# Queries taken from the key products, kept in DRAM, and three more exp buffers in a two-layer attention kernel

## The chip, the core and the metric

The kernel runs on one core of one Trainium2 chip. The metric is the device time of one execution in microseconds; 1635.77 us is the median of three runs of the kernel before.

## What is computed

Two layers, each an attention block and a feed-forward block on the same weights, with x of 2048 rows of 512 values in bf16:

```python
x = A_x
x = x + _A_ref(_layernorm(x, axis=-1), A_wqkv, A_wo)
x = x + _B_ref(_layernorm(x, axis=-1), B_w1, B_w2)
x = x + _A_ref(_layernorm(x, axis=-1), A_wqkv, A_wo)
x = x + _B_ref(_layernorm(x, axis=-1), B_w1, B_w2)
```

`_A_ref` is full softmax attention with 32 heads of 16 dimensions and no mask: scores are q k^T / 4, 2048 by 2048 for each head, then the product with v, then the output weights wo. `_B_ref` is x w1 (512 to 1792), silu, and w2 back to 512.

## The kernel before, in words

**Tiles and segments.** The heads are taken in 8 blocks (`hb`) of four, the queries in 4 chunks (`c`) of 512. A *segment* is one chunk of queries for one head block in one layer. Its work is cut into tiles of 128 keys (`kt`) by two heads by 512 queries: a score matmul pair writes a PSUM slot of 128x1024 (L1244; there are three slots), an exp takes the slot to an SBUF buffer in bf16, and value matmuls (L1320) add the buffer into the PSUM bank of the segment. There are 74 segments and 2048 tiles. Layer 1 starts on its first two chunks before the last quarter of the keys exists: kinds "old" (24 tiles) and "new" (8 tiles) share the work of a chunk, and the "old" sum is kept and rescaled by `f_piece` when the "new" part is done.

**Two ways to do an exp.** ScalarE (ACT) does it in one activation (L1459). VectorE (DVE) does it by bits: a tensor_scalar that writes 16-bit integers that read as bf16 (L1489), and three more copies of these shifted by constants, whose average is close to the exp. The shifts are done by GpSimd (POOL, L1550) or at times by DVE (L1523). A tile that DVE takes holds four buffers and needs four value products instead of one.

**Who orders the work.** A planner in the kernel's own Python code (`Flow`) plays the engines' clocks with fixed costs and writes the order of PE, ACT, DVE and POOL out; the chip follows that order, with semaphores where one engine needs another. `want_dve` gives a tile to DVE only if enough exp buffers are free (`spare`), not too many shifts are in arrears (`behind`), not too many rows wait for their value product (`ROWS`), and DVE is not late (`LATE`). The five thresholds `spare, many, few, behind, hurry` come from a table `KINDS` with a letter for each setting; `RULES` gives a letter to every stretch of 16 tiles. Work other than scores and values (projections, feed-forward, layer norms) is cut into `Piece`s, lists of steps with an engine, a cost and a due time, in four queues. Steps named "sp" are issued as soon as what they follow is done, and their DMAs land on the planner's clock after `T_ISSUE` and `T_LAND`. `warm` lets PE do matmuls on idle data (L1355) where its busy share in the last 3.3 us would fall below 0.65. DMAs on SP's queue are issued in the program's order.

**Exp buffers.** `bufs` holds NB = 11 of them; `lent` adds storage that is idle for a while: the four pairs of `q_old` and eight pieces of layer 1's value rows early in layer 0 (given back at segments 8, 15, 16, 24 and 32), the idle hidden tile for a few segments, and twelve more from segment 59 on.

**Keys and queries.** `wkq` holds the weights of keys and queries woven head by head: 16 columns of keys, then 16 of queries. A key product (`k_piece`, four steps of four matmuls, L306) takes 128 of these columns, so that its PSUM bank holds, for each of the four heads, 16 rows of keys and 16 rows of queries. `k_out` (L315) keeps the keys, multiplies the query rows by zero, and adds a row of ones:

```python
nc.vector.tensor_scalar(
    out=KT[:, hb, c * 512 : (c + 1) * 512], in0=ps,
    scalar1=own, scalar2=onescol, op0=ALU.mult, op1=ALU.add,
)
```

A query product (`q_mm`) takes the same columns moved on by 16, so that the queries fall on the keys' rows. `q_own` (L381) masks it into `qc`, `q_abs` (L388) takes absolute values, `q_abs_bias` (L396) makes a weight from the largest keys, a bias product on PE (`q_bias`) turns them into a bound on each score, and `q_sum` (L405) writes query and bound to the tile that the scores read. These steps are one chain: only one segment's chain runs at a time. `q_old` keeps the queries of the "old" segments (and those of layer 0's last chunk, made a chunk ahead) for the "new" ones; `q_again` (L454, L464) makes the new query tile from it.

**Transposes** of outputs and activations are DMAs on SP's queue (`turn`, L234).

Of the kernel before, what the change touches and what calls it, by code (L numbers as in the profile page):

```python
# [20 lines left out]
def kernel(  # L21
# [16 lines left out]
    P = 128  # L38
# [24 lines left out]
    NB = 11  # L63
# [12 lines left out]
    small = ctx.enter_context(tc.tile_pool(name="small", bufs=2))  # L76
    spool = ctx.enter_context(tc.tile_pool(name="spool", bufs=3, space=bass.MemoryType.PSUM))
# [96 lines left out]
    KT = xpool.tile([P, HB, S], BF16, name="KT")  # L174
    amax = xpool.tile([P, HB, NQC], FP32, name="amax")
# [3 lines left out]
    q_old = xpool.tile([P, HB, 512], BF16, name="q_old")  # L179
    q_more = xpool.tile([P, 512], BF16, name="q_more")  # L180
# [5 lines left out]
    q_mores = [q_more[:], v_flat[:, 1024 * HB : 1024 * HB + 512]]  # L186

# [3 lines left out]
    def q_kept(seg):  # L191
        return q_old[:, seg.hb, :] if seg.c != 1 else q_mores[MORE.index(seg.hb)]
# [37 lines left out]
    turns = [0]  # L230

    def turn(out, in_):
        turns[0] += 1
        nc.sync.dma_start_transpose(out=out, in_=in_)  # L234

# [8 lines left out]
    class Piece:  # L244
        def __init__(self, steps, after=None, lag=0):
            self.steps, self.lag = list(steps), lag
            self.after = list(after) if isinstance(after, (list, tuple)) else [after] * (after is not None)
            self.due = 0
            self.chain = None
# [129 lines left out]
    def q_own(ps):  # L379
        qc = qwork.tile([P, 512], BF16, name="qc", tag="qc")  # L380
        nc.vector.tensor_scalar(  # L381
            out=qc[:], in0=ps, scalar1=own, scalar2=None, op0=ALU.mult
        )
        return qc
# [38 lines left out]
    def q_pieces(seg, after):  # L423
        cell = {}

        def c1():
            cell["qc"] = q_own(cell["ps"][:, :])

        def c2():
            cell["qu"] = q_abs(cell["qc"])  # L430

        def d():
            bank(cell, "q_ps")
            q_bias(cell["bm"], cell["ps"][:, :], cell["qu"])

        def e():
            dst = q_kept(seg) if seg.keep else q_tile()
            q_sum(cell["ps"][:, :], cell["qc"], dst)
            seg.QT = dst

        first = Piece(four(
            lambda cts: q_mm(seg.c, seg.hb, cell["ps"][:, :], cts),
            lambda: bank(cell, "q_ps"),
        ) + [dve(750, c1, "c"), dve(302, c2, "l")])
        bm = bound(seg, cell, after)
        last = Piece([pe(MM, d, "o"), dve(700, e, "c")], [first, bm])
        return chained(first, bm, last, cell)

    def q_again(seg, after):
        cell = {}  # L450

        def a():
            cell["q"] = q_tile()
            nc.vector.tensor_scalar(  # L454
                out=cell["q"].bitcast(I16), in0=q_kept(seg).bitcast(I16),
                scalar1=0x7FFF, scalar2=None, op0=ALU.bitwise_and,
            )

        def b():
            bank(cell, "q_ps")  # L460
            q_bias(cell["bm"], cell["ps"][:, :], cell["q"])

        def e():
            nc.vector.tensor_tensor(  # L464
                out=cell["q"], in0=cell["ps"][:, :], in1=q_kept(seg), op=ALU.add
            )
            seg.QT = cell["q"]

        first = Piece([dve(302, a, "l")])
        bm = bound(seg, cell, after)  # L470
        last = Piece([pe(MM, b, "o"), dve(700, e, "c")], [first, bm])
        return chained(first, bm, last, cell)

    def f_piece(seg, after):

        cell = {}

        def a():
            cell["ps"] = narrow("f_ps")
            mm(cell["ps"][:, :], sel[:, 0, :], seg.QT, True, False)  # L480

        def b():
            mm(cell["ps"][:, :], sel[:, 1, :], q_kept(seg), False, True)
# [11 lines left out]
        return Piece([pe(MM, a, "o"), pe(MM, b), act(T_TANH, e, "c"), dve(690, m, "l")], after)  # L495
# [146 lines left out]
    def ending(oT, attn, slots, units):  # L642
# [90 lines left out]
        def hidden(f2):  # L733
            if f2 % 2 == 0:
                w = wide("h2_ps") if f2 else first
                pss = [w[:, i, :] for i in range(2)]
            else:
                pss = [p.tile([P, 512], FP32, name="h3_ps", tag=t)[:, :] for p, t in pools]
            for i in range(2):
                h_mm(c, 2 * f2 + i, pss[i], range(CT))  # L740
            for i in range(2):
                k = 2 * ((2 * f2 + i) % 4)
                t_sb = q_old[:, k : k + 2, :].bitcast(FP32).rearrange("p a b -> p (a b)")
                h_out(hT, 2 * f2 + i, pss[i], h_tanh(pss[i], t_sb))
# [21 lines left out]
    class Seg:  # L766
        def __init__(self, L, c, hb, kind):
# [3 lines left out]
            self.keep = kind == "old" or (L, c) == (0, NQC - 1)  # L771
# [36 lines left out]
    def old_keys(hb):  # L808
        new = [k_piece(c, hb) for c in range(NQC - 1)]
        for c, p in enumerate(new):  # L810
            p.after = [normed[c]] * (normed[c] is not None)
        first, rest = q_pieces(segs[NQC * HB + hb], None)
# [5 lines left out]
        rest[0].after = [parts[-1]]  # L818
        return [new[0], new[1], parts[0], first, new[2]] + parts[1:] + rest

    def prep(t):

        seg = segs[t]
        if seg.kind == "new" and seg.c == 1:
            first, rest = q_again(seg, None)
            return [first] + rest + [f_piece(seg, rest[-1])]
        if seg.kind == "new":
            new = []
            last = v_end[0] if v_end else None
            first, rest = q_again(seg, None)  # L830
            if seg.hb > 0:
                new = [k_piece(NQC - 1, seg.hb)]
# [4 lines left out]
            rest[0].after = [new[-1]]  # L837
            return [first] + new + rest + [f_piece(seg, rest[-1])]
        if seg.L == 0 and seg.c == 0:
            new = [k_piece(c, seg.hb) for c in range(NQC)]  # L840
            first, rest = q_pieces(seg, None)
# [6 lines left out]
            rest[0].after = [parts[-1]]  # L848
            return [new[0], new[1], parts[0], first, new[2], parts[1], new[3], parts[2], parts[3]] + rest
        if seg.kind == "old" and seg.c == 0:  # L850
            return old_keys(seg.hb) if seg.hb == HB - 1 else []
        first, rest = q_pieces(seg, None)
        return [first] + rest

    def musts(i):

        ts = list(range(i + 1 if i <= n_old else i + 2, i + 2 if i < n_old else i + 3))
        if (segs[i].L, segs[i].c) == (0, NQC - 2):
            ts.append(i + HB)
        last = (NQC - 1) * HB  # L860
        return [
            p for t in ts if t < len(segs) and not (last <= t < last + HB and t != i + HB)
# [6 lines left out]
    k_ns = ns_of([k_piece(0, 0)])  # L869
# [39 lines left out]
    def old_rows():  # L909
        return [q_old[:, 2 * k : 2 * k + 2, :] for k in range(HB // 2)]  # L910

    done = n_old + 2 + 2 * HB
    lent = [
        (0, 2 * HB - 1, spare(old_rows)),
# [5 lines left out]
        (done, 99, spare(old_rows)),  # L920
# [3 lines left out]
    class Flow:  # L924
# [40 lines left out]
        def landed(self, at):  # L965
            n, turns[0] = turns[0], 0
            for _ in range(n):
                start = max(self.sp, at + 100)
                self.sp = start + T_ISSUE
                at = max(at, start + T_LAND)  # L970
            return at
# [3 lines left out]
        def head(self):  # L975

            for q in self.qs:
                while q and not q[0].begun and q[0].steps[0][0] == "dve":
                    self.bg.append(q.pop(0))
            for q in self.qs:  # L980
                if q and q[0].steps[0][0] == "sp" and all(d.done for d in q[0].after):
                    p = q.pop(0)
# [118 lines left out]

        def begin(self, seg):
# [3 lines left out]
            if seg.L == 0 and seg.c == NQC - 1 and seg.hb > 0:  # L1106
                new = due(old_keys(seg.hb - 1), first[NQC * HB + seg.hb - 1])
# [4 lines left out]
            self.qs[0] += v_late * (i == 0) + musts(i)  # L1112
# [17 lines left out]
        def close(self):  # L1130
# [22 lines left out]
            if oT is not None:  # L1153
# [23 lines left out]
                if seg.hb == HB - 1:  # L1177
# [5 lines left out]
                    if seg.L == 0:  # L1183
                        new += next_pieces(seg.c, 1, ln, new[-1])
                        if seg.c == NQC - 1:
                            new.append(k_piece(seg.c, 0))
# [4 lines left out]
                    self.qs[1] += due(new, first[end] - 8)  # L1191
# [397 lines left out]
    RULES = (  # L1589
        "llllllllllllllllwwwwaaaaaaaaaaaaaaaajjjjaaaaaaaabbbbaaaaaaaaaaaa"  # L1590
        "aaaaaaaaaaaaaaaaaaaaaaaaaaaaaaaaffffffffffffffffmmmmmmmmcccccccc"
    )
# [156 lines left out]
```

## Time and profile before

| what | before |
|---|---|
| median of three runs, us | 1635.77 (1634.13 to 1635.88) |
| the profiled execution's own time, us | 1633.4 |
| its span, first to last instruction, us | 1631.6 |
| first score / first exp on ACT, us | 32.1 / 32.7 |
| last exp on ACT ends, us | 1589.1 |
| tiles with their exp on ACT / on DVE | 1625 / 423 |
| shifts on POOL / on DVE | 1155 / 114 |
| DMA transposes on SP | 139 |
| granted TensorE clock | 0.998 |

An engine's busy time on the page is the union of its instructions' times. Matmuls overlap: four of 32 columns run side by side, and the next four start 0.226 us after them, though each is shown with 0.38 us. ACT's exps overlap as well: one is shown with 1.19 us and the next starts after 0.917 us. A row of the groups gives the line, the engine, out<-in by the program's names (with shapes), the count, the busy time and the mean duration, then the engine's idle time just before these instructions and what ended it. A row of a table by stage gives the stretch, its length, then busy time (count) of the instructions asked for, the granted clock, the share of the DMA engines and GB/s.

### The profile page before, as it was taken

What the parts mean: (1) busy time and instruction counts of PE and PEld (TensorE: products, weight loads), DVE (VectorE), ACT (ScalarE), POOL (GpSimd) and SP (SyncE); (2) the same over time, 40 slices, a digit from 0 to 9 for tenths busy, and PEclk for the clock granted to TensorE, in tenths of its full rate; (3) what the DMA queues carried; (4) which work ended last, traced back from release to release, by engine and by line L of the source; (5) the groups of instructions that cost most, each with busy time, mean ns of one, the idle gap of its engine ahead of it and who ended that gap; (6) DMA issues with size and microseconds to landing.
All of it is one profiled execution on the core that took longest, in us unless ns stands there. A gap on an engine that the chain in (4) does not pass through costs nothing.

```text
span 1631.6 us, 42640 instructions
## 1 busy us (share of the span) xinstructions
PE 1558.9 (96%) x17522; PEld 498.3 (31%) x17528; DVE 1177.3 (72%) x1481; ACT 1582.1 (97%) x1796; POOL 1239.4 (76%) x1305
## 2 busy tenths in 40 slices
PE   8999999999999999999999998999999999999998
PEld 3232222223323333233333233222223322333333
DVE  7788888776777767657886557787666787777754
ACT  6999999999999999999999999999999999999993
POOL 3899998886788778766766655877767889889970
PEclk9999999999999999999999999999999999999999
DMA  5000001000110011001000000001000100010010
GB/s 194 5 8 8 8 8 24 15 8 12 28 21 5 8 27 28 5 8 18 21 14 2 1 15 8 11 11 30 17 8 14 24 21 8 12 37 11 8 28 13
DMA packets 85268, 30.80 MB, mean 19 GB/s; under 512 B 76624, under 2 KB 84560, under 8 KB 85072
## 3 DMA queue, kind: packets, MB, share of 16 engines
q1 hardware_dynamic: 83056, 26.99, 7.2%
q8 instruction: 137, 2.24, 0.6%
q10 hardware_dynamic: 2016, 1.08, 0.2%
q14 instruction: 59, 0.48, 0.1%
HBM read 7.86 MB, written 2.10 MB: 6 GB/s over the span
## 4 chain that ended last, share of the span: by engine, by line
PE 59%; ACT 19%; DVE 9%; issue 6%; POOL 5%; DMA 1%; ACTq 0%; DVEq 0%; POOLq 0%
PE slot L1244 20%; PE q_ps L1320 17%; ACT p L1459 13%; PE y_ps L306 7%; PE q_ps L306 3%; POOL p L1550 3%; PE h_ps L306 3%; PE k_ps L306 3%; ACT t_sb L568 2%; DVE p L1489 2%; ACT v L1459 2%; DVE hT L572 1%; PE v_ps L306 1%; POOL v L1550 1%; DVE attn L502 1%
## 5 line engine op out<-in xcount | busy, mean ns | idle before, releaser
L1459 ACT ACTIVATE p<-slot 128x1024 bf16<-128x1024 f32 x1171 | 1166.7, 1191 | 8.7 <-PE slot L1244 7.9
L1550 POOL TENSOR_TENSOR p<-p,steps 128x512 int32<-128x512 int32 x568 | 594.8, 1071 | 229.3 <-DVE p L1489 195.1
L1320 PE MATMUL q_ps<-p,v 128*17 128x512 bf16 x4634 | 527.3, 381 | 5.4 <-POOL p L1550 2.1
L1244 PE MATMUL slot<-QT,KT 32*128 32x512 bf16 x3104 | 439.5, 382 | 22.2 <-ACT p L1459 7.5
L1489 DVE TENSOR_SCALAR p<-slot 128x1024 uint16<-128x1024 f32 x281 | 342.7, 1220 | 118.1 <-PE slot L1244 112.2
L1244 PEld LDWEIGHTS <-KT 32*128 32x128 bf16 x4096 | 190.0, 91 | 579.0 <-issue 572.9
L1459 ACT ACTIVATE v<-slot 128x1024 bf16<-128x1024 f32 x301 | 338.7, 1210 | 1.4 <-PE slot L1244 1.2
L1320 PEld LDWEIGHTS <-v 128*17 128x17 bf16 x6634 | 162.5, 88 | 283.8 <-issue 224.7
L1320 PE MATMUL q_ps<-v,v 128*17 128x512 bf16 x1308 | 201.4, 381 | 1.1 <-DVE oT L1146 0.4
L1550 POOL TENSOR_TENSOR p<-v,steps 128x512 int32<-128x512 int32 x162 | 170.8, 1075 | 26.8 <-DVE v L1489 22.7
L1550 POOL TENSOR_TENSOR v<-p,steps 128x512 int32<-128x512 int32 x127 | 135.3, 1072 | 25.7 <-DVE p L1489 19.8
L1459 ACT ACTIVATE q_old<-slot 128x1024 bf16<-128x1024 f32 x129 | 149.0, 1197 | 0.6 <-PE slot L1244 0.5
L1489 DVE TENSOR_SCALAR v<-slot 128x1024 uint16<-128x1024 f32 x93 | 113.4, 1220 | 39.5 <-PE slot L1244 35.9
L306 PE MATMUL h_ps<-xnT,w_sb 128*32 128x512 bf16 x1568 | 129.0, 384 | 12.7 <-DVE hT L572 9.7
L1244 PE MATMUL slot<-q_old,KT 32*128 32x512 bf16 x896 | 122.7, 382 | 4.6 <-ACT p L1459 2.9
L572 DVE SCALAR_TENSOR_TENSOR hT<-t_sb,h_ps 128x512 bf16<-128x512 f32 x98 | 67.0, 684 | 77.9 <-ACT t_sb L568 77.9
L306 PE MATMUL y_ps<-w_sb,hT 128*32 128x512 bf16 x1568 | 120.4, 382 | 1.0 <-DVE hT L572 0.6
L1320 PE MATMUL q_ps<-q_old,v 128*17 128x512 bf16 x582 | 95.3, 381 | 0.2 <-DVE oT L1146 0.2
L306 PE MATMUL q_ps<-xnT,wkq 128*32 128x512 bf16 x1008 | 82.9, 383 | 2.2 <-DVE hT L572 1.7
L306 PE MATMUL k_ps<-xnT,wkq 128*32 128x512 bf16 x960 | 77.5, 383 | 1.7 <-DVE hT L572 0.7
L568 ACT ACTIVATE t_sb<-h_ps 128x512 f32<-128x512 f32 x98 | 73.9, 754 | 0.0
L1550 POOL TENSOR_TENSOR q_old<-p,steps 128x512 int32<-128x512 int32 x59 | 62.9, 1068 | 13.7 <-DVE p L1489 8.3
(162 smaller groups left out, 1532.2 us busy)
## 6 DMA issues: line engine op xcount, KB each, us to landing
w_sb<-in_B_w_dram SPq DMA_DIRECT2D x2, 1792.0 KB, 12.6
out_dram<-x_sb SPq DMA_DIRECT2D x15, 128.0 KB, 1.7
x_sb<-in_A_x_dram SPq DMA_DIRECT2D x3, 512.0 KB, 6.7
at<-oT SPq DMA_TRANSPOSE x63, 2.3
wraw<-in_A_wqkv_dram SPq DMA_DIRECT2D x2, 432.0 KB, 8.3
xnT<-hT SPq DMA_TRANSPOSE x44, 2.4
wv_sb<-in_A_wqkv_dram ACTq DMA_DIRECT2D x1, 512.0 KB, 6.3
wo_sb<-in_A_wo_dram SPq DMA_DIRECT2D x1, 512.0 KB, 8.2
```

The costliest lines, as they stand in the source:

```text
L306: nc.tensor.matmul(ps[g, :], lhsT=lhsT[:, g], rhs=rhs, start=start, stop=stop, skip_group_check=True)
L502: nc.vector.tensor_tensor(out=attn[:, :, 64 * hb : 64 * hb + DH * n].rearrange("p t (j d) -> p t j d", j=n), in0=at_ps[:, :, :, 0:DH], in1 ...
L568: nc.scalar.activation(t_sb, ps, ACT.Tanh, scale=0.5)
L572: nc.vector.scalar_tensor_tensor(out=hT[:, ft, :], in0=t_sb, scalar=1.0, in1=ps, op0=ALU.add, op1=ALU.mult)
L1244: nc.tensor.matmul(self.slots[k][:, jj, :], lhsT=KT[32 * j : 32 * j + KR, t.seg.hb, t.kt * P : (t.kt + 1) * P], rhs=t.seg.QT[32 * j : 32 * ...
L1320: nc.tensor.matmul(self.o_ps[32 * j : 32 * j + VW, :], lhsT=vs[seg.L][:, t.kt, 4 * seg.hb + j, :], rhs=buf[:, jj, :], start=not seg.opened ...
L1459: nc.scalar.activation(buf[:].rearrange("p a b -> p (a b)"), self.slots[x.slot][:].rearrange("p a b -> p (a b)"), ACT.Exp, scale=float(SCALE),
L1489: nc.vector.tensor_scalar(out=whole.bitcast(U16), in0=self.slots[x.slot][:].rearrange("p a b -> p (a b)"), scalar1=float(UNIT), scalar2=fl ...
L1550: nc.gpsimd.tensor_tensor(out=b1.bitcast(I32), in0=b0.bitcast(I32), in1=steps32[:, k : k + 1].to_broadcast([P, 512]), op=ALU.add,)
```

## The change

- A key product's bank is copied whole to a staging tile. Four DMAs of 16 rows take the keys of the four heads to KT, four more take the queries to a scratch in DRAM (`kept_q`). KT's other rows are filled once, by GpSimd, ahead of its other work (head blocks 1 to 7).
- Query products go, but for head block 0 of layer 0. A segment's chain begins with four loads from the scratch into `qc`, whose other rows stay zero. `q_again` goes: the "new" segments load the same queries again.
- `q_old` and `q_more` go. The finished query tile of an "old" segment is stored to DRAM (`old_q`) and fetched for `f_piece`. Layer 0's last chunk no longer makes its queries a chunk ahead.
- Exp buffers: 14 instead of 11. `q_old` is no longer lent; the value weights (2 buffers, from segment 45) and the woven key and query weights (4, from segment 53) are.
- Every stretch has the setting "a". The planner knows the moves' costs, and DMAs that one step issues no longer wait for each other's landing on its clock.

The core of the diff:

```diff
-    NB = 11
+    M_ISSUE, M_LAND = 100, 2200
+    NB = 14
...
     KT = xpool.tile([P, HB, S], BF16, name="KT")
+    for hb in range(1, HB):
+        nc.gpsimd.tensor_copy(out=KT[:, hb, :], in_=onescol.to_broadcast([P, S]))
...
+    def move(out, in_):
+        turns.append((M_ISSUE, M_LAND))
+        nc.sync.dma_start(out=out, in_=in_)
+
+    def groups(t, lo, cols):
+        return [t[32 * j + lo : 32 * j + lo + DH, cols] for j in range(4)]
...
-    def k_piece(c, hb):
+    def k_piece(L, c, hb):
         cell = {}
-        return Piece(four(
+
+        def out():
+            st = stpool.tile([P, 512], BF16, name="kq", tag="kq")
+            nc.vector.tensor_copy(out=st[:], in_=cell["ps"][:, :])
+            for k_in, k_to in zip(
+                groups(st, 0, slice(0, 512)), groups(KT[:, hb, :], 0, slice(512 * c, 512 * c + 512))
+            ):
+                move(k_to, k_in)
+            for j, q_in in enumerate(groups(st, DH, slice(0, 512))):
+                move(kept_q[L, hb, c, j, :, :], q_in)
+
+        p = Piece(four(
             lambda cts: k_mm(c, hb, cell["ps"][:, :], cts),
             lambda: bank(cell, "k_ps"),
-        ) + [dve(810, lambda: k_out(c, hb, cell["ps"][:, :]), "c")])
+        ) + [dve(700, out, "c")])
...
+        def load():
+            for j, q_to in enumerate(groups(qc, 0, slice(0, 512))):
+                move(q_to, kept_q[seg.L, seg.hb, seg.c, j, :, :])
+
+        if (seg.L, seg.hb) == (0, 0):
+            first = Piece(four(
+                lambda cts: q_mm(seg.c, seg.hb, cell["ps"][:, :], cts),
+                lambda: bank(cell, "q_ps"),
+            ) + [dve(750, c1, "c"), dve(302, c2, "l")])
+        else:
+            first = Piece([("sp", 0, load, "")], made)
+            first.chain = cell
+            first = Piece([dve(302, c2, "l")], first)
         bm = bound(seg, cell, after)
         last = Piece([pe(MM, d, "o"), dve(700, e, "c")], [first, bm])
...
-        (0, 2 * HB - 1, spare(old_rows)),
...
-        (done, 99, spare(old_rows)),
+        (n_old + 4, 99, spare(wv_rows)),
+        (keyed, 99, spare(key_rows)),
...
-    RULES = (
-        "llllllllllllllllwwwwaaaaaaaaaaaaaaaajjjjaaaaaaaabbbbaaaaaaaaaaaa"
-        "aaaaaaaaaaaaaaaaaaaaaaaaaaaaaaaaffffffffffffffffmmmmmmmmcccccccc"
-    )
+    RULES = "a" * (len(tiles) // STRETCH)
```

The letters are, in the order `spare, many, few, behind, hurry`: a (5, 6, 2, 3, 1.0), l (6, 9, 2, 3, 1.0), w (4, 6, 2, 5, 1.0), j (6, 4, 2, 3, 1.0), b (3, 4, 2, 3, 1.0), f (4, 6, 2, 3, 1.0), m (7, 4, 2, 3, 1.0), c (3, 6, 2, 3, 1.0).

More of the change, by code (lines that the diff above doesn't have):

```diff
@@ L436, in e @@
         def e():
[L437 to L444, printed above, removed]
+            seg.QT = q_tile()
+            q_sum(cell["ps"][:, :], qc, seg.QT)
+            if seg.kind == "old":
+                move(old_q[seg.c, seg.hb, :, :], seg.QT)
+        def load():
[10 more added lines that the diff above has]
+            first = Piece([dve(302, c2, "l")], first)
         bm = bound(seg, cell, after)
         last = Piece([pe(MM, d, "o"), dve(700, e, "c")], [first, bm])
[L447 to L456, printed above, removed]
-            )
[L459 to L472, printed above, removed]
+        head = first.after if made is not None else []
+        first, rest = chained(first, bm, last, cell)
+        return head + [first], rest
     def f_piece(seg, after):
@@ L493, in m, with load @@
             seg.scaled = True
-        return Piece([pe(MM, a, "o"), pe(MM, b), act(T_TANH, e, "c"), dve(690, m, "l")], after)
+        def load():
+            move(q_was[:], old_q[seg.c, seg.hb, :, :])
+        fetch = Piece([("sp", 0, load, "")])
+        f = Piece([pe(MM, a, "o"), pe(MM, b), act(T_TANH, e, "c"), dve(690, m, "l")], [fetch, after])
+        fetch.key, f.key = "fetch", "f"
+        return fetch, f
     def heads_norm(at_ps, hb, attn):
@@ L808, in old_keys @@
     def old_keys(hb):
-        new = [k_piece(c, hb) for c in range(NQC - 1)]
+        new = [k_piece(1, c, hb) for c in range(NQC - 1)]
         for c, p in enumerate(new):
             p.after = [normed[c]] * (normed[c] is not None)
-        first, rest = q_pieces(segs[NQC * HB + hb], None)
         parts = [
@@ L817, in old_keys @@
         parts.append(amax_all(hb, 2, parts))
-        rest[0].after = [parts[-1]]
-        return [new[0], new[1], parts[0], first, new[2]] + parts[1:] + rest
+        parts[-1].key = hb
+        return [new[0], new[1], parts[0], new[2]] + parts[1:]
     def prep(t):
@@ L907, in idle_hidden, with wv_rows, key_rows @@
         return [t[:, 2 * k : 2 * k + 2, :] for k in range(FT // 2)]
-    def old_rows():
-        return [q_old[:, 2 * k : 2 * k + 2, :] for k in range(HB // 2)]
+    def wv_rows():
+        assert all((1, tt) in v_made for tt in range(TT))
+        return [wv_sb[:, 2 * k : 2 * k + 2, :] for k in range(CT // 2)]
+    def key_rows():
+        assert with_q[1, NQC - 1, HB - 1].done
+        return [wkq[:, ct, 0 : 2 * D].rearrange("p (a b) -> p a b", a=2) for ct in range(CT)]
     done = n_old + 2 + 2 * HB
+    keyed = max(s.i for s in segs if s.kind == "new" and s.c == 0) + 1
     lent = [
-        (0, 2 * HB - 1, spare(old_rows)),
         (0, HB, spare(rows(x_flat, 0, 3))),
@@ L965, in landed @@
         def landed(self, at):
-            n, turns[0] = turns[0], 0
-            for _ in range(n):
+            land = at
+            for issue, ns in turns:
                 start = max(self.sp, at + 100)
-                self.sp = start + T_ISSUE
-                at = max(at, start + T_LAND)
-            return at
+                self.sp = start + issue
+                land = max(land, start + ns)
+            turns.clear()
+            return land
         def head(self):
             for q in self.qs:
[L978 to L982, printed above, removed]
+                while q:
+                    p = q[0]
+                    if p.steps[0][0] == "dve" and not p.begun:
+                        self.bg.append(q.pop(0))
+                        continue
+                    if p.steps[0][0] != "sp" or not all(d.done for d in p.after):
+                        break
+                    if p.chain is not None and self.chain not in (None, p.chain):
+                        break
+                    q.pop(0)
+                    self.chain = p.chain or self.chain
                     at = max([d.ready for d in p.after] + [min(self.pe, self.act, self.dve)])
@@ L1098, in force, with known @@
                 self.step(p, max(at, getattr(self, p.steps[0][0])))
+        def known(self, pieces):
+            for p in pieces:
+                if p.key == "fetch":
+                    p.after += [with_q[k] for k in ("f",) if k in with_q]
+                if p.key is not None:
+                    with_q[p.key] = p
+            return pieces
         def begin(self, seg):
```

80 lines of the change are left out of this document (42 added, 38 removed).

## The prediction, made before the changed kernel was run

> **What bounds the kernel now.** I read the page's busy line and its costliest groups first, then what ScalarE and VectorE wait for, then the exp instructions by stage.
>
> ```profile
> PE 1558.9 (96%) x17522; PEld 498.3 (31%) x17528; DVE 1177.3 (72%) x1481; ACT 1582.1 (97%) x1796; POOL 1239.4 (76%) x1305
> ...
> L1459 ACT ACTIVATE p<-slot 128x1024 bf16<-128x1024 f32 x1171 | 1166.7, 1191 | 8.7 <-PE slot L1244 7.9
> ```
>
> And from the groups of TensorE alone:
>
> ```profile
> L1355 PE MATMUL q_ps<-wo_sb,wkq 128*16 128x512 bf16 (+1 forms) x175 | 60.6, 379 | 0.0
> ```
>
> Both PE and ACT look full, but they are not full in the same way. L1355 issues matmuls that compute nothing: the planner puts them in where TensorE would otherwise idle. So the busy PE has room, and its chain share (59% of the span) mostly says that it hands ACT its slots on time. ACT has no such filler: before its largest group of exps it idles 8.7 us in 1631.6 us. Exps start on ACT every 0.917 us (mean distance of starts in the trace, gaps over 1.3 us left out). The trace has 1171 + 301 + 129 + 24 = 1625 exps on ACT, and 1625 x 0.917 = 1490 us. The other 423 of 2048 tiles go to DVE (L1489). **The time is therefore the number of tiles left to ACT:** each tile more on DVE is worth 0.92 us, if nobody makes ACT wait.
>
> What sets that number? I cut the trace where the lent exp buffers change (start of segments 8, 16, 24, 32, 42, 59, 66), and asked for L1489 in each stretch. The count in brackets is DVE's tiles.
>
> ```profile
> 32.10:215.50 183.40, 69.46 (x57) 1.00 0.04 7
> 215.50:403.70 188.20, 71.98 (x59) 1.00 0.06 13
> 403.70:601.30 197.60, 62.17 (x51) 1.00 0.09 17
> 601.30:798.60 197.30, 59.80 (x49) 1.00 0.08 16
> 798.60:990.00 191.40, 48.83 (x40) 1.00 0.05 11
> 990.00:1234.00 244.00, 69.42 (x57) 0.99 0.07 14
> 1234.00:1400.20 166.20, 62.23 (x51) 1.00 0.08 17
> 1400.20:1631.60 231.40, 72.04 (x59) 1.00 0.08 19
> ```
>
> The stretches hold 256, 256, 256, 256, 240, 304, 224 and 256 tiles, so DVE's shares are .223, .230, .199, .191, .167, .188, .228, .230. The buffers by the code are 23, 20, 14, 12, 11, 11 (18 for five short segments), 23, 23. The share follows the buffers up to about 20 and then stays. POOL agrees: its passes (L1550) fill 165 of 183 us in the first stretch and 116 of 191 us in the fifth.
>
> **The change, part by part.**
>
> *Buffers.* NB goes from 11 to 14, but q_old no longer lends its four; weights lend two, later six, late in layer 1. By stretch: 22, 19, 17, 15, 14, then 14 to 23 (mostly 16 to 23), then 28 and 28. I interpolate the shares above: 17 buffers lie halfway between 14 (.199) and 20 (.230), so .2145, 55 tiles for 51; 15 buffers .204, 52 for 49; 14 buffers .199, 48 for 40; about 17 buffers in the sixth, .2145, 65 for 57. The first two and the last two are on the flat part: 0. Together 4 + 3 + 8 + 8 = 23 tiles, x 0.92 = **-21 us**. Bounds: 0 (another condition holds DVE back) and 46 tiles, -42 us (all of segments 16 to 58 at .230).
>
> *Query products.* What goes is seen in the groups of TensorE and of VectorE:
>
> ```profile
> L306 PE MATMUL q_ps<-xnT,wkq 128*32 128x512 bf16 x1008 | 82.9, 383 | 2.2 <-DVE hT L572 1.7 <-DVE x_sb L581 0.2 <-DVE QT L405 0.2
> ```
>
> ```profile
> L315 DVE TENSOR_SCALAR KT<-k_ps,cols 128x512 bf16<-128x512 f32 x61 | 49.1, 806 | 13.1 <-PE k_ps L306 12.0 <-PE k_ps L302 0.5
> ...
> L381 DVE TENSOR_SCALAR qc<-q_ps,cols 128x512 bf16<-128x512 f32 x64 | 47.7, 746 | 12.8 <-PE q_ps L306 12.2
> ```
>
> 1008 matmuls are 63 products of 16. Three stay (head block 0 of layer 0), 60 go: 240 groups of four at 0.226 us (start to start in the trace) is 54 us of PE. On DVE 60 x 0.746 = 44.8 us go with L381, and 60 key evictions fall from 0.806 to the 0.69 of a plain copy out of PSUM (L1146: 0.685), 7.0 us. PE's part by itself is worth nothing, since its slack is already filled with idle matmuls. It also covers what more DVE tiles need: three more rows each, half a 0.22 us slot a row, 0.33 us. DVE's 51.8 us would be room for 36 tiles (1.22 us and 114 helper passes x 0.75 us over 423 tiles, 1.42 us each), if DVE's time were what refuses a tile. But DVE has 450 us idle now. I take 4 tiles, **-4 us**; bounds 0 and 36 tiles, -33 us. POOL must do 2.73 passes of 1.04 us a tile, 2.84 us: 27 tiles are 77 us of its 392 idle.
>
> *Moves.* 60 key pieces x 8, 70 segments x 4 loads, 10 stores and 10 fetches: 780 DMAs on SP's queue, which had 139 transposes. No move of 16 rows is in this trace. The nearest rows are the output stores of 128 rows:
>
> ```profile
> L586 SPq DMA_DIRECT2D out_dram<-x_sb x12: 332/348/577, 1246.9 to 1583.5; - x12
> ...
> DMA to landing us min/median/max: 1.7/1.8/2.1
> ```
>
> Issue is at most 780 x 0.35 = 273 us of SP, beside 139 x 1.2 us of transposes: SP stays under a third. Landing is 1.7 to 2.1 us for that store and 2.7 us for the load of 128 rows at the start; the planner reckons 2.2 us and 0.1 us of issue. With 0.35 us the fourth load lands 0.75 us later than planned. What waits is DVE's abs, and behind it in DVE's order evictions and DVE tiles; PE's bias product waits for the abs. ACT feels it only after the slot in hand, 0.92 us. Lower end: below nothing by a few us (the planner used to chain the transposes' landings one after the other and now overlaps them, which is nearer the trace's four in 5.1 us), upper 70 x 0.5 = +35 us. I take **+3 us**, nearest to the case in which the idle quarter of DVE absorbs it.
>
> The Trainium skill ("DMA: Bandwidth & Descriptors", section "Two DMAs through the same engine are not ordered") has a rule against a scratch in DRAM: a load that reads what an earlier DMA wrote must wait on the issuing engine for that DMA's semaphore. No row here has a store read back. Where a chain loads right behind its store (segments of the first chunk), SP would hold everything behind it for one landing, 1.8 us by the store's row, some 14 us of SP over seven segments and next to none of ACT's time.
>
> *KT's fill.* Seven broadcasts of 128x2048 on POOL, ahead of all passes. Nearest row: eight key copies of 432 columns.
>
> ```profile
> 14.38 4.27 POOL L155 COPY wkq<-wraw 128x432 bf16<-128x432 bf16 x8 [2.99 <-DMA wraw<-in_A_wqkv_dram]
> 38.38 2.04 POOL L1550 TENSOR_TENSOR p<-p,steps 128x512 int32<-128x512 int32 x2 [19.73 <-DVE p L1489]
> ```
>
> 0.53 us for 432 columns makes 2.5 us for 2048, 17.5 us for seven, inside the 19.7 us that POOL idles: 0. At the rate of the int32 add (1.07 us for 512) it is 30 us, 10 us late, and passes of the first segment wait. I take **+1**, bounds 0 and 10.
>
> *Thresholds.* 68 of the 128 letters are "a" already. Stretches 1, 7 and 8, mostly other letters, have .223 to .230 with the same 23 buffers, so a letter is worth at most .007, and over the 960 tiles that change letter 7 tiles, 6 us either way. The letter w (more passes in arrears) stands where DVE did most of its helper passes (28 in the second stretch): I take 3 tiles lost, **+3**; bounds -6 and +12, twice the spread.
>
> *The rest* (query tiles written to one place, fetches for the ten rescalings) has the same DVE and PE instructions as before, or fewer: 0.
>
> **Sum.** -21 - 4 + 3 + 1 + 3 = -18 on the profiled 1633.4 us (span 1631.6 and 1.8 around it), 1615.4. The median of the runs is 2.4 above the profiled one: **1618 us**.
>
> **Rivals.**
> 1. *DVE's freed time becomes tiles too:* 36 instead of 4, 29 us more, 1589. For it: DVE is 78% busy in the first stretch (143.8 of 183.4) where the share is flat. Against: there POOL is at 90%.
> 2. *The change doesn't do what it says:* the share does not follow the buffers, no tile moves. Then 1618 + 25 = 1643, or 1636 if the three costs are nil as well. For it: shares at 20 and 23 buffers are equal, and stretches also differ in feed-forward work.
> 3. *Landings take the place of the products (slower):* if moves are issued at 0.35 us and land over 0.6 us behind the plan, the in-order DVE and PE stand at each of 70 query chains, and ACT runs dry once its slot in hand is spent: 0.5 us each, 35 us, 1653. Against: a query chain is queued a segment (24 us) ahead, and DVE idles 28%.
> 4. *The one setting costs more:* its upper end and a little, 10 us more, 1628.
>
> **How the numbers follow.** Chances: forecast 0.45, first rival 0.20, second 0.12, third 0.15, fourth 0.08. 0.2% of 1636 is 3.3 us, about what a measurement here tells from no change. Faster: 0.45 + 0.20 + 0.05 of the fourth = 0.70. Same: 0.05 of the second and 0.03 of the fourth, 0.08. Slower: 0.15 and 0.07 of the second, 0.22. The range reaches from the first rival, 1589, to the second with a part of the third, 1650: beyond lie some 0.1 of the third and 0.05 below the first.
>
> **What would show it.** Right: L1489's successor near 450 instances, most of the growth between the starts of segments 16 and 59, and ACT's exps still 0.917 us apart. Moves: issue under 0.35 us and landing near 2 us; DVE's wait for loads into qc under 0.5 us each. Fill: POOL's first pass still near 38 us. Wrong: L1489 near 423 (second rival), or ACT idle by tens of us behind PE's slots, with PE or DVE waiting for DMAs (third), or near 485 instances (first).

## The result, and the profile after

The changed kernel takes 1766.49 us (median of four runs, 1760.83 to 1769.28) beside 1635.47 us for the kernel before on the same chips: a ratio of 1.0798, 95% interval 1.077 to 1.0827. It is 8% slower; the prediction was 1618 us with a range of 1589 to 1650. The profiled execution took 1767.64 us, its span is 1765.8 us.

The page's busy line, and the tiles on DVE (L1528 is the line that was L1489) by the same stretches, cut at the starts of the same segments:

```profile
PE 1608.9 (91%) x16823; PEld 488.4 (28%) x16829; DVE 1195.0 (68%) x1500; ACT 1571.0 (89%) x1769; POOL 1288.2 (73%) x1341
```

```profile
41.60:289.60 248.00, 69.44 (x57) 0.82 0.09 22
289.60:480.10 190.50, 69.63 (x57) 1.00 0.09 18
480.10:668.80 188.70, 69.61 (x57) 1.00 0.08 18
668.80:882.80 214.00, 64.68 (x53) 0.94 0.10 22
882.80:1115.10 232.30, 56.18 (x46) 0.90 0.11 27
1115.10:1366.60 251.50, 80.46 (x66) 0.97 0.12 27
1366.60:1532.30 165.70, 66.05 (x54) 0.99 0.10 20
1532.30:1765.80 233.50, 73.25 (x60) 0.99 0.09 20
```

The counts add up to 450 tiles, 27 more than before, and ACT has 11 us less to do. But ACT's share of the span fell from 97% to 89%: somebody makes it wait. The lengths of the stretches say where. The third became shorter (188.7 us for 197.6). The first grew by 65 us, the fourth by 17, the fifth by 41, the sixth by 8, and the first score starts 9.5 us later. The first, fourth, fifth and sixth are the stretches in which key pieces are made (28, 11, 14 and 7 of the 60). The others have only query loads, and apart from the third they stay within 2.3 us of before.

Three of the waits of the changed kernel, out of the list that begins with the longest (engine and line, what ended the wait, us in total, times, longest):

```profile
...
ACT p L1498 <- PE slot L1283: 103.2, 91, 6.2
DVE amax L356 <- DMA KT<-kq: 80.2, 34, 5.1
...
DVE kq L338 <- DMA kept_q<-kq: 25.5, 18, 3.8
```

ACT waits for scores, and DVE waits for the key moves before it can take the keys' maximum. The moves' issuing line on SP (count: shortest/median/longest in ns) and the landing of all moves:

```profile
L241 SPq DMA_DIRECT2D qc<-kept_q x280: 302/411/1767, 77.2 to 1676.9; - x140
L241 SPq DMA_DIRECT2D KT<-kq x240: 512/585/1701, 71.6 to 1225.2; - x120
L241 SPq DMA_DIRECT2D kept_q<-kq x240: 310/418/1660, 74.5 to 1227.4; - x120
...
DMA to landing us min/median/max: 1.5/1.7/3.6
```

Landing, 1.7 us in the median, is shorter than the planner's 2.2 us. Issue is not: SP spends 0.585 us on a key move and 0.418 us on a store (medians), where the planner reckons 0.1 us, so the eight moves of a piece take 4.0 us of SP. Here is one such place, from the timeline of the changed kernel (start, length, what, and in brackets how long the engine was idle before it and what ended that):

```profile
116.98 0.69 DVE L338 CAST kq<-k_ps 128x512 bf16<-128x512 f32 x1 [3.15 <-DMA kept_q<-kq]
...
118.36 1.96 SPq L241 DMA_DIRECT2D kept_q<-kq  x4
...
120.42 3.52 SPq L241 DMA_DIRECT2D KT<-kq  x4
...
125.28 0.69 DVE L356 TENSOR_REDUCE amax<-KT 128x1 f32<-128x512 bf16 x1 [4.56 <-DMA KT<-kq]
...
127.15 0.60 PE L1359 MATMUL q_ps<-p,v 128*17 128x512 bf16 x2 [2.74 <-DVE amax L363]
...
128.75 1.94 ACT L1498 ACTIVATE p<-slot 128x1024 bf16<-128x1024 f32 x2 [3.27 <-PE slot L1283]
```

The copy to the staging tile (first line) ended at 117.67. SP was issuing the moves of the piece before, the four stores in the second line being the last, until 120.32, and came to the four key moves only then; here they took 0.88 us each. DVE stands 4.56 us for them, with tiles and evictions queued behind; then PE, then ACT. The granted clock falls to 0.82 in this stretch, where PE is busy for 206 of 248 us (before: 1.00, and 179 of 183 us). In e2, without the key moves, it is 1.00 in the same stretch, so the low clock comes with the moves and is no cause apart from them. How much it adds to their cost was not taken apart.

### The profile page after: what moved, and what is told of

It is laid out like the page before. It is cut to its first block, busy times and chain, and to the rows that moved or that the text cites. A ratio compares the mean times of both kernels' runs of the same rounds, so it can differ in the third digit from the quotient of the medians.

```text
span 1765.8 us, 42538 instructions
## 1 busy us (share of the span) xinstructions
PE 1608.9 (91%) x16823; PEld 488.4 (28%) x16829; DVE 1195.0 (68%) x1500; ACT 1571.0 (89%) x1769; POOL 1288.2 (73%) x1341
## 4 chain that ended last, share of the span: by engine, by line
PE 46%; ACT 17%; DVE 12%; SPq 9%; issue 7%; DMA 5%; POOL 3%; DVEq 0%; ACTq 0%; POOLq 0%
PE slot L1283 16%; PE q_ps L1359 14%; ACT p L1498 11%; SPq L241 8%; PE y_ps L316 5%; PE h_ps L316 3%; DVE p L1528 3%; ACT v L1498 3%; DMA KT<-kq 3%; POOL p L1589 2%; ACT t_sb L587 2%; PE v_ps L316 1%; PE q_ps L1394 1%; DVE hT L591 1%; PE q_ps L316 1%
## 5 line engine op out<-in xcount | busy, mean ns | idle before, releaser
L1589 POOL TENSOR_TENSOR p<-p,steps 128x512 int32<-128x512 int32 x646 | 676.2, 1069 | 281.2 <-DVE p L1528 241.1
L1283 PE MATMUL slot<-QT,KT 32*128 32x512 bf16 x4096 | 597.3, 397 | 49.5 <-ACT p L1498 15.9
L1359 PE MATMUL q_ps<-p,v 128*17 128x512 bf16 x4970 | 585.3, 399 | 24.2 <-DVE p L1528 12.1
L1528 DVE TENSOR_SCALAR p<-slot 128x1024 uint16<-128x1024 f32 x324 | 395.5, 1221 | 158.2 <-PE slot L1283 145.4
L1283 PEld LDWEIGHTS <-KT 32*128 32x128 bf16 x4096 | 188.7, 91 | 637.0 <-issue 628.9
L1498 ACT ACTIVATE v<-slot 128x1024 bf16<-128x1024 f32 x283 | 314.4, 1181 | 32.5 <-PE slot L1283 32.4
L1589 POOL TENSOR_TENSOR p<-v,steps 128x512 int32<-128x512 int32 x142 | 151.1, 1080 | 28.5 <-DVE v L1528 28.4
L1528 DVE TENSOR_SCALAR v<-slot 128x1024 uint16<-128x1024 f32 x87 | 106.2, 1221 | 41.4 <-PE slot L1283 39.2
L356 DVE TENSOR_REDUCE amax<-KT 128x1 f32<-128x512 bf16 (+1 forms) x49 | 41.5, 847 | 81.4 <-DMA KT<-kq 80.2
L1394 PE MATMUL q_ps<-wo_sb,wkq 128*16 128x512 bf16 (+1 forms) x207 | 76.5, 399 | 0.0
L1498 ACT ACTIVATE wkq<-slot 128x1024 bf16<-128x1024 f32 x63 | 73.3, 1205 | 1.2 <-PE slot L1283 1.2
L1562 DVE TENSOR_SCALAR p<-p 128x1024 int16<-128x1024 int16 x97 | 72.9, 755 | 1.6
L338 DVE CAST kq<-k_ps 128x512 bf16<-128x512 f32 x60 | 41.3, 688 | 43.0 <-DMA kept_q<-kq 25.5
## 6 DMA issues: line engine op xcount, KB each, us to landing
w_sb<-in_B_w_dram SPq DMA_DIRECT2D x2, 1792.0 KB, 12.6
```

Source lines behind the costliest of these rows:

```text
L356: nc.vector.tensor_reduce(out=amax[:, hb, part : part + 1], in_=KT[:, hb, t0:t1], axis=AX.X, op=ALU.max, apply_absolute_value=True,)
L1283: nc.tensor.matmul(self.slots[k][:, jj, :], lhsT=KT[32 * j : 32 * j + KR, t.seg.hb, t.kt * P : (t.kt + 1) * P], rhs=t.seg.QT[32 * j : 32 * ...
L1359: nc.tensor.matmul(self.o_ps[32 * j : 32 * j + VW, :], lhsT=vs[seg.L][:, t.kt, 4 * seg.hb + j, :], rhs=buf[:, jj, :], start=not seg.opened ...
L1394: nc.tensor.matmul(out[0:DH, :], lhsT=wkq[rows, 0, 2 * D : 2 * D + DH], rhs=wo_sb[rows, 0, :], start=out is not self.o_ps, stop=out is not ...
L1498: nc.scalar.activation(buf[:].rearrange("p a b -> p (a b)"), self.slots[x.slot][:].rearrange("p a b -> p (a b)"), ACT.Exp, scale=float(SCALE),
L1528: nc.vector.tensor_scalar(out=whole.bitcast(U16), in0=self.slots[x.slot][:].rearrange("p a b -> p (a b)"), scalar1=float(UNIT), scalar2=fl ...
```

## The experiments

Each ratio is to the kernel before on the same chip. The totals are medians; the stage times are those of the profiled execution, from first score to first score, in us, for the segments named.

| run | total | to first score | 0-7 | 8-23 | 24-31 | 32-41 | 42-58 | 59 to end | tiles on DVE |
|---|---|---|---|---|---|---|---|---|---|
| before | 1635 | 32.1 | 183.4 | 386.0 | 197.3 | 191.4 | 243.9 | 397.5 | 423 |
| after | 1766 | 41.6 | 248.0 | 379.3 | 213.9 | 232.4 | 251.3 | 399.1 | 450 |
| e1 told | 1863 | 40.2 | 277.8 | 382.9 | 212.0 | 285.2 | 266.2 | 396.9 | 446 |
| e2 keys by DVE | 1668 | 32.0 | 188.1 | 384.4 | 194.1 | 215.7 | 250.1 | 401.3 | 443 |
| e3 few moves | 1675 | 31.2 | 186.6 | 379.3 | 195.0 | 231.9 | 251.1 | 396.1 | 450 |
| e4 before, setting a | 1645 | 32.1 | 184.1 | 387.4 | 197.3 | 196.1 | 244.9 | 400.5 | 413 |
| e5 keys in one DMA | 1666 | 31.5 | 190.8 | 377.7 | 196.2 | 223.2 | 246.1 | 398.7 | 446 |
| e6 fill by DMA | 1756 | 31.5 | 247.3 | 379.5 | 210.6 | 234.1 | 252.1 | 397.6 | 450 |
| e7 few, spare 9 | 1633 | 32.1 | 188.4 | 382.1 | 194.4 | 195.7 | 237.4 | 401.5 | 430 |
| e8 few, 11 buffers | 1652 | 31.3 | 189.1 | 385.3 | 198.3 | 203.5 | 246.7 | 395.8 | 428 |
| e9 e5 + 6 idle moves | 1734 | 31.9 | 226.1 | 381.0 | 198.1 | 246.9 | 248.5 | 398.6 | 446 |
| e10 four staging tiles | 1759 | 40.0 | 247.6 | 379.9 | 214.9 | 227.2 | 247.5 | 400.5 | 448 |
| e11 e7, tuned | 1634 | 31.3 | 189.7 | 379.6 | 194.3 | 195.6 | 249.2 | 394.1 | 434 |
| e12 e5 + 8 idle moves | 1791 | 31.2 | 254.1 | 382.5 | 205.9 | 262.7 | 256.8 | 397.0 | 446 |

**e1, the planner told.** `M_ISSUE, M_LAND = 550, 1900` for `100, 2200`.

> The changed kernel with the planner told the moves' true price: issue 550 ns instead of 100, landing 1900 ns after issue begins instead of 2200. Nothing else changes. Theory (the order is written for moves that are issued in 0.1 us, and on the chip SP takes 0.58 us for a key move and 0.42 for a store, so keys land late and DVE stands in its order behind them): SP's true need in a segment of the first chunk is about 16 x 0.58 + 16 x 0.42 + 4 x 0.41 + 1.2 = 19 us of 24, so there is room, and an order that knows it gets most of the loss back: 1660 to 1700 us, DVE's wait for keys at the maximum of the keys well under half of its 80 us. Rival (SP's queue itself is the bound, whatever the order knows): 1740 us or more. Rival (KT's fill at the start): 9.5 us of the loss stay in either case.

1862.7 us, ratio 1.1399 (1.1382 to 1.1416). The theory failed in its second half. The order did take the price in: DVE's wait for keys at the maximum fell from 80.2 us to 3.7. But nothing came back. DVE's wait for stores, before it may write a staging tile again, grew from 25.5 us to 68.0, and a part of the waiting moved into the order: in segments 0 to 7 PE now runs 172 idle matmuls (L1394) instead of 19, and ACT is without scores for 7 to 9 us near the end of most of them.

```profile
DVE kq L338 <- DMA kept_q<-kq: 68.0, 19, 5.8
...
DVE amax L356 <- DMA KT<-kq: 3.7, 1, 3.7
```

So a planner told this pair of prices does no better while the moves must be made; other pairs were not tried.

**e2, keys by DVE; e3, few moves.** e2 replaces the key moves and the fill by the old `k_out`, a second eviction. e3 also makes the four stores one, and the four loads one; its copy to the staging tile keeps the query rows alone, by a mask:

```diff
-            nc.vector.tensor_copy(out=st[:], in_=cell["ps"][:, :])
-            for k_in, k_to in zip(
-                groups(st, 0, slice(0, 512)), groups(KT[:, hb, :], 0, slice(512 * c, 512 * c + 512))
-            ):
-                move(k_to, k_in)
-            for j, q_in in enumerate(groups(st, DH, slice(0, 512))):
-                move(kept_q[L, hb, c, j, :, :], q_in)
+            nc.vector.tensor_scalar(
+                out=st[:], in0=cell["ps"][:, :], scalar1=query, scalar2=None, op0=ALU.mult
+            )
+            move(kept_q[L, hb, c, :, :], st[DH:P, :])
...
-        ) + [dve(700, out, "c")])
+        ) + [dve(750, out), dve(810, lambda: k_out(c, hb, cell["ps"][:, :]), "c")])
...
-            for j, q_to in enumerate(groups(qc, 0, slice(0, 512))):
-                move(q_to, kept_q[seg.L, seg.hb, seg.c, j, :, :])
+            move(qc[0 : P - DH, :], kept_q[seg.L, seg.hb, seg.c, :, :])
```

> The changed kernel with the keys written to KT by DVE as before (0.81 us each) and no key moves and no fill of KT; queries still go to DRAM in four stores and come back in four loads. DVE has 60 x 0.81 = 49 us more than the changed kernel. Theory (late key moves): segments 0 to 7 fall from 248 us to under 200, the first score is back at 32 us, total 1640 to 1670. Rival (the round trip of the queries through DRAM is what is late): over 1720, and DVE waits for loads into qc by tens of us.

> As the kernel with keys by DVE, but the queries of a piece go to DRAM in one store of 112 rows (the copy keeps the query rows alone by a mask, 0.75 us instead of 0.69) and come back in one load of 112 rows: 130 moves instead of 760, and no fill of KT. Theory (the number of issues on SP): all the loss is gone and the 27 more tiles on DVE show: 1605 to 1625 us. Rival (the time of landing, which stays, or the thresholds): not below 1650.

e2: 1667.75 us, ratio 1.0209 (1.0192 to 1.0226). e3: 1674.92 us, 1.0246 (1.0231 to 1.0261). In segments 0 to 7 both are within 5 us of before, so 60 of the 65 us lost there go with the key moves; the queries' round trip through DRAM is not late. Of the 131 us that the changed kernel lost, e2 gives 99 back. But e3 missed its total by 50 us, and 130 key and query moves are no better than 520. Its loss stands in one place. Timelines of e3, TensorE with SP, and ACT:

```profile
989.01 19.44 PE L1389 MATMUL w_ps<-wo_sb,wkq 128*16 128x512 bf16 x45 [0.34 <-DVE x_sb L595]
...
993.27 5.12 SPq L236 DMA_TRANSPOSE xnT<-hT  x4
1008.50 1.05 PE L315 MATMUL v_ps<-wv_sb,xnT 128*32 128x512 bf16 x16
```

```profile
1025.38 2.85 ACT L1493 ACTIVATE p<-slot 128x1024 bf16<-128x1024 f32 x3 [38.88 <-PE slot L1278]
```

ACT is idle for 38.9 us at the end of segment 41. The "new" segments need chunk 3's last keys, and these its feed-forward block, whose products end at 988 us; then come normalization, transposes, values, keys and a query chain, with nothing else left to do: PE runs 45 idle matmuls. Before, the same products ended at 965 us, 25 us ahead of segment 42. Not all of e3's gap is this chain: its transposes have landed by 999.5 us, and the first value product stands behind idle matmuls of the order until 1008.5. In e2, e5 and e8 it follows the landing by 1 to 3 us.

**e4, the thresholds alone**, on the kernel before.

> The kernel before with the setting a in every stretch, nothing else. The prediction's term: 3 us, between -6 and +12, so 1630 to 1648. Rival (the thresholds are a large part of the loss): over 1670.

1644.51 us, ratio 1.0058 (1.0043 to 1.0073): about 9.5 us, and 10 tiles fewer on DVE.

**e5, the keys by one DMA.** DVE writes masked keys and ones to a staging tile `sk`, and `move(KT[:, hb, 512 * c : 512 * c + 512], sk[:])` takes all 128 rows.

> As e3_few_moves, but the keys go to KT by a DMA again: DVE writes keys and ones into a staging tile (0.81 us), and one DMA of 128 rows takes it to KT, so a key piece issues 2 moves, where the changed kernel issues 8 and e3 one. 13 buffers instead of 14, for the staging tiles' room. Theory (what costs segments 0 to 7 their 65 us is the serial issue of eight moves on SP, 4 us a piece): segments 0 to 7 take 185 to 200 us, total within 15 us of e3. Rival (it is the landing of a key DMA, near 2 us each, however few they are): segments 0 to 7 over 225 us, total 1710 or more.

1666.37 us, ratio 1.0197 (1.0181 to 1.0214); segments 0 to 7 take 190.8 us. The keys still land 2.0 us after issue, but DVE's wait for them at the maximum is 4.2 us in the whole kernel, where it was 80.2: landing costs little, and the number of moves is what costs.

**e6, the fill.** `nc.sync.dma_start` of 128x512 for each chunk and head block instead of the GpSimd copies.

> The changed kernel with KT's other rows filled by 28 DMAs of 128x512 from one tile of 512 columns, instead of by seven GpSimd copies of 1.88 us. Theory (DVE's normalizations L228 stand behind the GpSimd copies, four in 7.29 us where they took 1.38): the first score comes at 32 to 33 us instead of 41.6, total 1755 to 1762. Rival (the late start has another cause, the loads or the clock): first score still near 41.

1756.09 us, ratio 1.0751 (1.0731 to 1.0771), and the first score at 31.5 us. GpSimd in the changed kernel, then DVE there, and DVE in e6:

```profile
19.10 13.19 POOL L179 CAST KT<-cols 128x2048 bf16<-128x2048 f32 x7
```

```profile
25.15 7.29 DVE L228 TENSOR_SCALAR v<-x_sb,mvb,rstd 128x512 bf16<-128x512 bf16 x4
```

```profile
23.43 1.38 DVE L230 TENSOR_SCALAR v<-x_sb,mvb,rstd 128x512 bf16<-128x512 bf16 x4
```

The fill does fit into GpSimd's idle time, as the prediction had it, but each of these four DVE instructions takes about as long as one GpSimd copy, 1.88 us. The Trainium skill ("SBUF — State Buffer", section "Who interferes with whom") says that GpSimd and a DVE instruction in one of its two-port modes share a pair of ports, which one of them holds for a whole instruction while the other is blocked. The two traces fit this: 1.82 us each beside the copies and 0.35 without, while the statistics instructions (L201) beside the same copies keep their 0.66 to 0.68 us. The traces do not name the mode.

**e7 and e8, why segment 41 stalls.** e7 is e3 with the planner told the moves' price (350 and 2000 ns) and `RULES = "a" * 64 + "B" * 16 + "a" * 48`, where B is (9, 4, 2, 3, 1.4). e8 is e3 with `NB = 11`.

> As e3_few_moves, with the planner told these moves' price (350 ns issue, 2000 ns landing), and in the 16 stretches of the old segments (32 to 41) a setting that asks for 9 free buffers before DVE takes a tile, and 1.4 times the pace of other work. Theory (e2 and e3 lose 26 to 39 us in one piece at segment 41, where chunk 3's feed-forward is late, because DVE takes 6 to 9 tiles more in the old segments and the feed-forward needs DVE too): no gap of ACT over 10 us, segments 32 to 41 near 195 us instead of 232, total 1630 to 1645 with fewer tiles on DVE. Rival (landing times or the queries made in that stage hold the feed-forward back): a gap of 25 us or more stays, total over 1660.

> e3_few_moves with 11 exp buffers instead of 14. If the three buffers' tiles are worth 0.92 us each wherever they fall, about 22 tiles fewer make it 1695. Theory (tiles gained in the old segments only lengthen the wait for chunk 3's keys): the gap at segment 41 shrinks by 10 us or more, and the total is 1660 to 1675, no slower than e3.

e7: 1633.02 us, ratio 0.9989 (0.9978 to 1.0), with no gap of ACT over 4.1 us. DVE takes 34 tiles in the old segments instead of 49, and the stretch is 36 us shorter. e8: 1652.09 us, 1.0106 (1.0088 to 1.0124), better than the 1660 us at which its range began; 22 tiles fewer on DVE, and 23 us faster than e3, with the gap down from 38.9 to 8.6 us. Chunk 3's last feed-forward products end 171 us after the start of the old segments in e8, with 39 tiles on DVE there, 196 us in e3 with 49, 192 in e5 with 45, 183 in e2 with 46, 164 in e7 with 34, and 167 before with 40. So in segments 32 to 41 of this kernel a further tile on DVE does not save 0.92 us; it puts off the feed-forward that the next stage waits for. That they compete for DVE's time is my reading of this; e8 changes the number of buffers and nothing else. e7 changes the pace of other work and the moves' prices with the threshold; how much of its gain is each one's was not taken apart.

**e9 and e12, idle moves added.** e5 with `nc.sync.dma_start(out=junk[L, hb, c, j, :, :], in_=sk[0:DH, :])` six or eight times ahead of each key move, in e5's order.

> e5_keys_one_dma with six more DMAs of 16 rows issued ahead of each key move, from the staging tile into a DRAM tile that nothing reads; the planner is not told of them, so the order of all other work is that of e5. A key piece then issues 8 moves, as in the changed kernel, and its keys' own move is the seventh. Theory (serial issue on SP): the time of segments 0 to 7 comes back, 225 to 255 us instead of 191, and the total is 1730 to 1790. Rival (issue on SP is free, what matters is how the keys are split or landed): within 10 us of e5.

> e9_dummy6 with eight idle moves a key piece instead of six. In a segment of the first chunk SP is then issuing for 4 x (0.52 + 8 x 0.42 + 0.47) + 0.31 + 1.2 = 18.9 us, as long as in the changed kernel (4 x (4 x 0.585 + 4 x 0.418) + 4 x 0.41 + 1.2 = 18.9 us); with six it was 15.6 us. Theory (the time that SP spends issuing in these segments sets their length): segments 0 to 7 take 240 to 256 us, like the changed kernel's 248, after 226 with six and 191 with none. Rival (a part of the changed kernel's loss in these segments has another cause, such as four landings to wait for instead of one): 226 to 238 us.

e9: 1733.75 us, ratio 1.062 (1.0598 to 1.0642). e12: 1790.55 us, 1.0951 (1.0932 to 1.0969). Nothing reads what these moves write, and the keys' own move is e5's. DVE's wait for the keys in e12:

```profile
DVE amax L362 <- DMA KT<-sk: 117.1, 41, 6.8
```

In segments 0 to 7 SP's DMA instructions, transposes included, add up to 20 us in e3, 34 in e5, 69 in e2, 118 in e9, 142 in the changed kernel and 141 in e12, and the stretch takes 187, 191, 188, 226, 248 and 254 us: the changed kernel lies within 6 us of the one with the same issuing time. The transfers themselves are not the cause: a key move lands 2.0 us after issue (median) in e5, e9 and e12 alike, and the DMA engines' share in this stretch is 0.18 in e12 and 0.09 in the changed kernel, which takes nearly as long. e9's total came out at the low end of its expectation, its stretch at 226.

**e10, four staging tiles** instead of two (`stpool` with `bufs=4`, 13 exp buffers).

> The changed kernel with four staging tiles for key products instead of two (and 13 exp buffers instead of 14, for their room). DVE waits 25 us for stores before it may write a staging tile again, and TensorE stands behind it. If that wait is a cost of its own, 15 us or more come back, 1750 or less. Theory (it is the same queue of moves, met at another place): less than 10 us either way, 1756 to 1776, and the wait for keys at the maximum grows.

1759.11 us, ratio 1.076 (1.0733 to 1.0788). The wait for stores ahead of the staging copy goes, and the wait at the keys' maximum grows from 80.2 us to 105.5: the same queue, met elsewhere.

**e11, a try at a faster version:** e7 with settings of its own after segment 41, C (7, 9, 2, 4, 1.0) for 16 stretches and D (6, 6, 2, 4, 1.0) for the last 32.

> e7_few_spare9 with settings of their own after segment 41: spare 7, many 9, behind 4 in the next 16 stretches, and spare 6, many 6, behind 4 in the last 32. The planner's rule about arrears lets DVE take tiles more often late in the kernel. Expected 2 to 9 us under e7, 1624 to 1631, which would be faster than the kernel before by 0.2 to 0.6%. If e7's order is already at the limit of its engines, no change.

1633.95 us, ratio 0.9995 (0.9983 to 1.0006): no change, where 1624 to 1631 was expected, though DVE takes 4 tiles more than in e7. No version here beats the kernel before beyond the measurement.

## Why the prediction was wrong

**What bounds the kernel, and the buffers: right in kind.** 450 tiles on DVE were forecast (423 + 27) and 450 came; by stretch 57, 53, 46 and 66 in the four that were to gain, for 55, 52, 48 and 65. That the total fits to the tile is in part luck: four of the 27 were to come from DVE's freed time, the sum took three off again for the thresholds, and e4 shows ten lost by these. The buffers' own term was 23 tiles, and e8 shows 22 for three buffers. Where nothing else went wrong the gain showed: segments 16 to 23 became 8.9 us shorter for 6 tiles, which at 0.92 us are 5.5. The step that failed is "if nobody makes ACT wait", taken as a condition and then not checked stage by stage. e8 shows the further error: in the old segments a tile on DVE is worth less than nothing; by my reading because the feed-forward that the next stage waits for needs DVE as well. The prediction cut the trace into stages for the buffers, and did not ask which work must end with each stage.

**The moves: the third rival's kind of mechanism, priced too low and put at the wrong place.** The term was +3 us with an upper end of +35. The issue was taken as 0.35 us a move at most, 273 us in all; it came as 0.411, 0.418 and 0.585 us by kind (medians), 384 us in all. "SP stays under a third" held as an average over the span (579 of 1766 us), and says nothing of a stage: in the first eight segments SP issues for 142 of 248 us, and in bursts of eight. The step that failed is the wait. I counted the key piece's eight moves into SP's load, but took a wait only for the query chain's four loads, though the keys have a chain of their own: moves, maximum, bound, query tile. Without the key moves (e2) segments 0 to 7 are 60 us shorter, and 24 to 31 are 20 us shorter. The loads, which I did price, cost little: DVE's wait for `qc` is 11.4 us in all. I also took landing for the risk; at 1.5 to 1.8 us it came as forecast, and e5 and e9 show that it is issue. The loads right behind their stores, for which I set aside some 14 us of SP (seven times 1.8 is 12.6), cost nothing: in the changed kernel's trace SP waits for no store to `kept_q`. The sign named for this rival came: ACT idle by tens of us behind PE's slots, with DVE waiting for DMAs.

**Telling the planner the price does not mend it:** with the issue and landing of e1 the kernel is 96 us slower still.

**Segments 32 to 41: +41 us, not fully taken apart.** Without the key moves the stretch is 17 us shorter in e2, but no shorter in e3, where the late feed-forward leaves a gap of 38.9 us. In e9 and e12 idle moves lengthen e5's stretch by 23.7 and 39.5 us and its gap of 27.5 us stays (27.5 and 28.4), so there the two add up. The changed kernel has many gaps, of 6.2 us and less, 38.6 us in all, and its last feed-forward products end 200 us after the start of the stretch, where it was 167. How much of its 41 us belongs to the moves and how much to DVE's tiles is not settled.

**KT's fill: +1 us was taken, with 10 as the upper end; 9.5 to 10 came.** The duration was forecast well (17.5 us taken, 30 at most, 13.2 measured) and the cover is there. The step that failed is "inside the 19.7 us that POOL idles: 0": I asked whether POOL had time and not what DVE was doing in it.

**The thresholds: +3 us and three tiles were taken, between -6 and +12 us; 9.5 us and ten tiles came (e4).** Mis-sized, inside its bounds.

**Query products: right that DVE's freed time makes few tiles, against the first rival.** In e3 DVE does two evictions for a key piece instead of one, and 450 tiles come all the same. That PE's part is worth nothing was not tested by itself; idle matmuls (L1394) rose from 175 to 207 in that group.

**Adding up, on the spans:** 9.5 (fill) + 64.6 (segments 0 to 7) + 16.6 (24 to 31) + 41.0 (32 to 41) + 7.4 (42 to 58) + 1.6 (the end) - 6.7 (8 to 23) = 134 us, for 1765.8 - 1631.6 = 134.2. The thresholds' 9.5 us and the tiles' gain are spread over these. The 7.4 us of 42 to 58 were not taken apart; e2 and e3 lose 6 and 7 us there too.

## What to carry to other kernels

Price a DMA's issue on its queue as an instruction of that engine, count the DMAs of one burst, and follow what waits for the burst's last one; a queue that is under a third busy on average can still set the length of a stage. Before an engine's time is counted as a gain, ask for each stage what must be finished at its end, because a faster supply of the main work only reaches that wait sooner. And when work goes into an engine's idle time, look at what its neighbours run in that same window.

## What the runs showed of the hardware that was not expected

- A DMA of 16 rows of 1 KB costs SP 0.585 us from SBUF to SBUF and 0.418 us to DRAM, about as much as one of 112 or 128 rows (0.30 to 0.60 us; medians by kind, the last one e6's fill). So fewer and larger moves cost SP less: in segments 0 to 7 e3's 35 moves take 11 us of it, the changed kernel's 252 take 133.
- A store of 16 KB to DRAM lands in 1.5 us and a load of it in 1.7 us, so the round trip itself was never the trouble.
- DVE's normalization takes 0.35 us alone and 1.8 us beside GpSimd copies of 1.88 us; its statistics instructions take 0.66 to 0.68 us in both cases.
